# Masked attention and a mixture of attention heads on one core: the weights' jobs five units further up, 65-wide slices of V, and a refitted order

## The chip, the cores and the metric

The kernel runs on one core of a Trainium2 chip. What is compared is device time in microseconds (us): the median of several runs of one launch. Times of single instructions come from one profiled execution.

## The reference, cut to what matters

```python
def reference(q, k, v, proj, w_gate, wq, wk, wv, wo):   # q, k, v: 4 x 8 x 768 x 64
    qb, kb = bucket(q @ proj), bucket(k @ proj)          # 6 sign bits each
    s = where(qb[..., :, None] == kb[..., None, :], q @ k.T / 8, -1e9)
    x = softmax(s) @ v                                   # 4 x 8 x 768 x 64
    x = x.transpose(0, 2, 1, 3).reshape(4, 768, 512)
    w, topk = softmax over the best 2 of 4 of x @ w_gate
    out = 0
    for e in range(4):                                   # wq, wk, wv: 4 x 512 x 64
        a = softmax(causal((x @ wq[e]) @ (x @ wk[e]).T / 8))
        out += (w of e, where e is in topk) * (a @ (x @ wv[e]) @ wo[e])
    return out                                           # 4 x 768 x 512
```

## The kernel before, in words

**Units.** The work is a list `seq` of 48 units: 32 of the masked attention (`L`, one per batch and head) and 16 of the mixture (`M`, one per batch and expert). A unit's scores are 768 x 768, made transposed in chunks of up to 512 columns: TensorE writes scores to PSUM (`st`), ScalarE takes their exponential twice, into `p` (float32) and `ph` (float16), GpSimd or VectorE writes the rest `pl` = p - ph, and TensorE multiplies by V in three matmuls per 128 x 128 block: `o<-vh,ph`, `o<-vl,ph`, `o<-vh,pl` (V too is split, `vh` + `vl`). VectorE then divides by the denominators into `xp` (`yn` in the mixture). Two units ahead TensorE makes the scores once more the other way round (`mx`), and VectorE reduces them to each row's maximum (`pm`, `pmw`), which goes by way of a small transposed row (`row`, `roww`) and a DMA into the scores' operand.

**Jobs beside the units.** Loads of a pair of heads (`natq`, `natk`, `natv`), their scales (`mqk`), their float16 halves (`qk`, `xt`), the hash signs (TensorE `misc<-qk,pbh` and `misc<-qk,pbl`, matmuls of 32 columns of weights that run four side by side in column groups; VectorE `M`), the preparation of V (`vf`, `vh`, `vl`, `vcol`, `vr`), the transposes of x (`xt`) and the mixture's projections. `load_weights` is a generator of nine steps: it stages the expert weights in `wst`, takes their largest magnitudes (`qkmax`, `mw`) on VectorE, scales them on ScalarE (`wst<-wst,cw`), and writes halves (`wqk_h`, `wvg_h`, `wo_h` on ScalarE, `wqk_l`, `wvg_l`, `wo_l` on GpSimd). The main loop counts units from -6; from unit `W0` on it runs one step of that generator per unit.

**What sets the order.** All operations are recorded first, in the loop's order. `schedule()` is a list scheduler: it gives each engine its instructions in the order of the recorded position plus a number for the operation's group out of the table `PLACE`, by a planner that costs each kind of operation from the table `TIMES` and waits by `LAT` and `LATE`. Some operations may go to either of two engines, and the planner chooses. `issue()` then emits them, so that in the profile every instruction carries one line (L716 before). Engines run their queues in order; SP (SyncE) issues nearly all DMAs. Fillers (`o<-ident`) are matmuls at the start, whose result nobody uses. Each of the three `st` tiles is one PSUM bank, and so are the two `misc`, the two `mx` and the one `o`.

**V's slices before.** A pair's V tile holds [unused, ones, V of head 0, V of head 1, ones] in 132 columns. Head 1 took the 65 columns from 66 on (V, ones); head 0 took 66 columns from 0 on, with V two columns in, so that its `o<-vl,ph` wrote from column 66i + 2 of the PSUM tile.

Of the kernel before, what the change touches and what calls it, by code (L numbers as in the profile page):

```python
# [133 lines left out]
class Op:  # L134
# [133 lines left out]
scalar activation lg misc 4 4 PS 151 258 0 0 0
scalar activation misc gw 24 24 SP 130 194 0 0 0
scalar activation misc lg 24 24 SP 102 197 0 0 0  # L270
scalar activation mvh misc 256 256 PS 276 383 0 0 0
scalar activation ot misc 512 512 PS 576 687 0 0 0
# [7 lines left out]
scalar activation pf st 512 512 PS 478 607 0 0 0  # L280
scalar activation ph st 256 256 PS 263 419 0 0 0
scalar activation ph st 384 384 PS 370 503 0 0 0
scalar activation ph st 512 512 PS 477 605 0 0 0
scalar activation qk misc 384 384 PS 372 490 0 0 0
scalar activation qk natk 384 384 SS 501 640 0 0 0
scalar activation qk natk 768 768 SS 895 1015 0 0 0
scalar activation qk natq 384 384 SS 498 619 0 0 0
scalar activation qk natq 768 768 SS 895 1015 0 0 0
scalar activation row misc 128 128 PS 158 256 0 0 0
scalar activation roww misc 128 128 PS 167 258 0 0 0  # L290
scalar activation rw cw 1 1 SS 147 242 0 0 0
scalar activation vcol misc 1 1 PS 53 178 0 0 0
scalar activation vf natv 384 384 SS 507 625 0 0 0
scalar activation vh vf 384 384 SS 419 550 0 0 0
# [170 lines left out]
class Recorder:  # L465
# [102 lines left out]
    def schedule(self):  # L568
# [39 lines left out]
        while left:  # L608
# [1285 lines left out]
```

## Time and profile before

| | |
|---|---|
| median of 3 runs | 607.84 us (606.49 to 609.29) |
| profiled execution, its own time | 609.53 us |
| its span, first to last instruction | 607.8 us (1.7 us of the time lie outside) |
| mean granted TensorE clock | 0.994 |
| busy, share of the span: PE, DVE, ACT, POOL | 98%, 82%, 83%, 76% |

PE is TensorE, PEld its weight loads, DVE VectorE, ACT ScalarE, POOL GpSimd. Matmuls overlap each other, so PE's busy time is time in which at least one is under way; how fast they follow one another is read from their starts.

### The profile page before, as it was taken

To read this page: it belongs to the slowest core of one execution; us is meant where nothing else is said; L and a number is where in the kernel's file an instruction comes from. 1 tells how busy PE (TensorE), PEld (TensorE's weight loads), DVE (VectorE), ACT (ScalarE), POOL (GpSimd) and SP (SyncE) were. 2 spreads that over 40 slices of the span, in tenths; PEclk is the share of its full clock that TensorE was granted. 3 is DMA by queue.
4 is the path that set the end of the run, shared out by engine and by line. 5 is a ranking of instruction groups with operands and counts; after the bars stand their busy time and mean duration, and the time that the engine had idled before them with its cause. 6 is when DMAs were issued, how large, how long until landed. Compare 5 with 4: busy or idle time off the path is not lost.

```text
span 607.8 us, 20469 instructions
## 1 busy us (share of the span) xinstructions
PE 593.4 (98%) x7850; PEld 429.4 (71%) x7850; DVE 499.0 (82%) x1374; ACT 502.1 (83%) x1075; POOL 463.1 (76%) x520
## 2 busy tenths in 40 slices
PE   8899999999999999999999999999999999999996
PEld 6567876667677776777776676767766767767673
DVE  5896889999899899988989789987979794557853
ACT  6586999999888899977997899887978978954683
POOL 9476798999965989985896689867996778951550
PEclk9997999999999999999999999999999999999999
DMA  5652064150422115131324314141033121011222
GB/s 170 164 166 67 9 173 138 42 151 18 140 80 94 45 42 138 25 115 42 105 61 131 104 44 132 28 132 35 19 124 99 50 63 28 11 27 43 57 89 104
DMA packets 38967, 50.24 MB, mean 83 GB/s; under 512 B 13226, under 2 KB 27350, under 8 KB 38870
## 3 DMA queue, kind: packets, MB, share of 16 engines
q1 hardware_dynamic: 38870, 48.95, 28.6%
q8 instruction: 61, 1.00, 0.7%
q14 instruction: 36, 0.29, 0.1%
HBM read 20.98 MB, written 6.29 MB: 45 GB/s over the span
## 4 chain that ended last, share of the span: by engine, by line
PE 83%; DVE 6%; ACT 5%; DMA 2%; issue 2%; POOL 1%; SPq 1%; ACTq 0%; POOLq 0%; DVEq 0%
PE misc L716 25%; PE st L716 25%; PE o L716 21%; PE mx L716 13%; ACT ph L716 2%; DVE pm L716 1%; ACT p L716 1%; DMA natv<-in_v_dram 1%; POOL pl L716 1%; DVE qk L716 1%; DVE xt L716 1%; SPq L716 1%; DMA wst<-in_moe_wk_dram 1%; DVE misc L716 1%; DMA xt<-roww 0%
## 5 line engine op out<-in xcount | busy, mean ns | idle before, releaser
L716 POOL TENSOR_TENSOR pl<-p,ph 128x512 f16<-128x512 f32 x367 | 409.0, 1141 | 116.6 <-ACT ph L716 44.6
L716 ACT ACTIVATE p<-st 128x512 f32<-128x512 f32 x372 | 227.7, 616 | 30.2 <-PE st L716 24.2
L716 PE MATMUL st<-qk 78*128 78x512 f16 (+3 forms) x976 | 228.1, 324 | 0.4
L716 ACT ACTIVATE ph<-st 128x512 f16<-128x512 f32 x372 | 228.0, 621 | 0.6 <-PE o L716 0.4
L716 DVE TENSOR_REDUCE pm<-mx 128x2 f32<-128x512 f32 (+2 forms) x284 | 186.9, 675 | 16.4 <-PE mx L716 15.2
L716 PEld LDWEIGHTS <-ph 128*128 128x128 f16 x2880 | 157.2, 98 | 25.0 <-DVE xp L716 1.5
L716 PEld LDWEIGHTS <-qk 128*128 128x128 f16 (+5 forms) x1560 | 130.0, 98 | 56.6 <-issue 7.0
L716 PEld LDWEIGHTS <-pl 128*128 128x128 f16 x1440 | 132.5, 97 | 9.8 <-POOL pl L716 4.2
L716 PE MATMUL mx<-qk 76*128 76x512 f16 (+2 forms) x488 | 135.6, 325 | 1.9 <-DVE pm L716 1.0
L716 PE MATMUL o<-vh,ph 128*128 128x65 f16 (+1 forms) x1104 | 126.9, 194 | 2.1 <-DVE xp L716 1.0
L716 PE MATMUL o<-vl,ph 128*128 128x64 f16 x1104 | 126.6, 192 | 0.1
L716 PE MATMUL o<-vh,pl 128*128 128x65 f16 (+1 forms) x1104 | 125.3, 194 | 0.5 <-POOL pl L716 0.3
L716 PE MATMUL misc<-xt,wqk_h 128*128 128x384 f16 x256 | 57.7, 325 | 0.2 <-DVE qk L716 0.2
L716 DVE CUSTOM_DVE_ANT_0 spare<-mx,causal 128x512 bf16<-128x512 f32 (+2 forms) x96 | 44.3, 461 | 9.3 <-PE mx L716 7.4
L716 PE MATMUL o<-mvh,pl 128*128 128x65 f16 x336 | 37.4, 193 | 0.8 <-POOL pl L716 0.8
L716 PEld LDWEIGHTS <-xt 128*128 128x128 f16 x324 | 30.3, 97 | 10.8 <-ACT xt L716 0.5
L716 PE MATMUL o<-mvh,ph 128*128 128x65 f16 x336 | 37.6, 194 | 0.0
L716 PE MATMUL o<-mvl,ph 128*128 128x64 f16 x336 | 37.6, 192 | 0.0
L716 PEld LDWEIGHTS <-wqk_h 128*128 128x128 f16 x256 | 24.1, 98 | 14.6 <-issue 0.3
L716 POOL TENSOR_TENSOR vl<-vf,vh 128x384 f16<-128x384 f32 x32 | 29.3, 925 | 6.0 <-DVE qk L716 2.6
L716 ACT ACTIVATE qk<-misc 128x384 f16<-128x384 f32 x26 | 13.0, 500 | 20.4 <-PE misc L716 20.2
L716 PE MATMUL misc<-wvg_h,xt 128*128 128x260 f16 x192 | 29.7, 274 | 0.0
(198 smaller groups left out, 902.9 us busy)
## 6 DMA issues: line engine op xcount, KB each, us to landing
qk<-qk SPq DMA_DIRECT2D x128, 96.0 KB
natv<-in_v_dram SPq DMA_DIRECT2D x16, 384.0 KB
qk<-qk SPq DMA_DIRECT2D x32, 192.0 KB
natq<-in_q_dram SPq DMA_DIRECT2D x15, 384.0 KB
natk<-in_k_dram SPq DMA_DIRECT2D x15, 384.0 KB
out_dram<-ot SPq DMA_DIRECT2D x20, 256.0 KB
xt<-xt SPq DMA_DIRECT2D x4, 192.0 KB
out_dram<-p SPq DMA_DIRECT2D x3, 256.0 KB
```

Of the source, the lines that this page charges most:

```text
L716: o.made = getattr(getattr(self.nc, e), m)(*[real(x) for x in args], **{k: real(x) for k, x in kw.items()})
```

## The change

The weights' generator starts at unit -2 and not 3. Both heads take V in slices 65 wide: head 0 from column 1 (ones, V), so that its moving operand starts at an odd float16 and its `o<-vl,ph` writes from column 66i + 1. All numbers of `PLACE` are new, and `TIMES` is measured anew (most entries move by a few per cent; a matmul in column groups falls from 60 to 40 ns). The planner counts what it costs TensorE to enter or leave the column groups (`TURN`), lets GpSimd wait out a VectorE operation that it is made to follow, and scales a landing's delay by the tile.

```diff
-W0 = 3
+W0 = -2
+TURN = 97.0
+CLASH = 0
-tensor matmul dt.float16 384 - g 60 326 0 0 0
+tensor matmul dt.float16 384 - g 40 326 0 0 1
...
+                    if e == "tensor" and mode and not a[4][4]:
+                        pen += TURN
...
-                st += pen if o.wide else 0.0
-                last = busy
+                st += pen + (TURN if port > mode else 0.0)
+                last, mode = busy, port
...
-                o.end += LATE
+                of = o.ins[0].tile.name.rstrip("0123456789_") if o.ins else ""
+                o.end += LATE * (1.5 if of in ("M", "Mw") else 0.4 if of in ("row", "roww", "fr", "vr", "rows") else 1.0)
...
                 if half is not None and hold[0] + 100.0 < st:
                     o.after, half = half, None
-                if hold[1] - 130.0 > st and hold[0] < st + 80.0:
+                    st = max(st, hold[1] + LAT[e])
+                elif hold[1] - 130.0 > st and hold[0] < st + 80.0:
                     st = hold[1] - 130.0
...
-            U["L", b, 2 * hp + h].update(vf=vf[:, :, 66 * h:66 * h + 66], vh=vh[:, :, 66 * h:66 * h + 66], vl=vl[:, :, h], first=2 - 2 * h, den=64 * h,
-                                         order=[2 * (i % 3) + i // 3 for i in range(NT)], c=c, vs=vs[:, h])
+            w = slice(1 + 65 * h, 66 + 65 * h)
+            U["L", b, 2 * hp + h].update(vf=vf[:, :, w], vh=vh[:, :, w], vl=vl[:, :, h], first=1 - h, den=64 * h,
+                                         order=[2 * (i % 3) + i // 3 for i in range(NT)], c=c, vs=vs.rearrange("p h d -> p (h d)")[:, w])
...
-                        w = 66 if f else 65
-                        oa, ol = O[:, 66 * i:66 * i + w], O[:, 66 * i + f:66 * i + f + 64]
+                        oa, ol = O[:, 66 * i:66 * i + 65], O[:, 66 * i + f:66 * i + f + 64]
```

The instructions stay the same in number but for 12 more fillers and some copies that change between VectorE and ScalarE. Their order is new on every engine. Three places show it.

On SP, the first DMAs after the first loads; `xt<-roww` carries the row maxima on which the first score chunk waits. Before:

```order
L716 DMA xt<-xt 64x384 x2
L716 DMA qk<-qk 64x384 x4
L716 DMA xt<-xt 64x768 x2
L716 DMA xt<-xt 64x384 x2
L716 DMA natv<-in_v_dram 128x768
L716 DMA xt<-roww 1x6x128
```

After:

```order
L720 DMA xt<-xt 64x384 x2
L720 DMA wst<-in_moe_wq_dram 128x4x64
L720 DMA qk<-qk 64x384 x4
L720 DMA xt<-xt 64x768 x2
L720 DMA xt<-xt 64x384
L720 DMA wst<-in_moe_wk_dram 128x4x64
L720 DMA natv<-in_v_dram 128x768
L720 DMA wst<-in_moe_wq_dram 128x4x64
L720 DMA xt<-xt 64x384
L720 DMA wst<-in_moe_wk_dram 128x4x64
L720 DMA xt<-roww 1x6x128
```

Four of the eight loads of wq and wk now stand between the start's own DMAs, ahead of `xt<-roww`; before, all eight stood behind the loads of a later pair of heads.

On VectorE, the place of the reductions `qkmax`. Before, they lie around the normalisation (`xp`) of the fifth masked unit, some 150 rows into the queue:

```order
L716 TENSOR_SCALAR rden<-o,cs_529 128x6
L716 RECIPROCAL cs_1846<-misc 128x1
L716 TENSOR_SCALAR negh_167<-misc 128x12
L716 RECIPROCAL rden<-rden 128x6
L716 TENSOR_REDUCE qkmax<-wst 128x2
L716 TENSOR_TENSOR xp<-o,rden 128x6x64
L716 TENSOR_REDUCE qkmax<-wst 128x2
L716 SCALAR_TENSOR_TENSOR qk<-natq,cs_1846,qk 128x2x384
```

After, they begin some fifteen rows into the queue, between the row maxima (`pmw`) of the second unit:

```order
L720 COPY least_times<-misc 128x3
L720 TENSOR_REDUCE pmw_184<-mx 128x2 x2
L720 TENSOR_REDUCE misc<-misc 128x1
L720 TENSOR_REDUCE qkmax<-wst 128x2
L720 TENSOR_SCALAR Mw<-misc,least_times 128x384
L720 TENSOR_REDUCE pmw_184<-mx 128x2
L720 TENSOR_SCALAR misc<-misc 128x1
```

So `xp` no longer stands behind a reduction of the weights, and the start's row maxima do.

On TensorE, the hash signs of a pair of heads (`misc<-qk,pbh` and `pbl`, 12 matmuls; the weight loads between them are single rows). Before, one such run is broken in two by a matmul of `mx` and a transpose of `vcol`:

```order
L716 MATMUL misc<-qk,pbl 32x384
L716 LDWEIGHTS pbl
L716 MATMUL misc<-qk,pbl 32x384
L716 LDWEIGHTS qk
L716 MATMUL mx<-qk 128x512
L716 MATMUL misc<-ident,vcol 1x128
L716 LDWEIGHTS pbl
L716 MATMUL misc<-qk,pbl 32x384
L716 LDWEIGHTS pbh
L716 MATMUL misc<-qk,pbh 32x384
```

After, the 12 stand together; this is the end of one run:

```order
L720 MATMUL misc<-qk,pbl 32x384
L720 LDWEIGHTS pbl
L720 MATMUL misc<-qk,pbl 32x384
L720 LDWEIGHTS pbh
L720 MATMUL misc<-qk,pbh 32x384
L720 LDWEIGHTS pbh
L720 MATMUL misc<-qk,pbh 32x384
L720 LDWEIGHTS qk
L720 MATMUL mx<-qk 128x512
```

In the whole program the column-group matmuls stand in 22 runs before and in 17 after.

## Rows read from the trace of the kernel before

**Rows 1.** Windows: length, then PE, PEld, DVE, ACT, POOL busy us, PEclk, DMA share, GB/s.
```profile
0.00:52.00 52.00, 46.92 (x446) 33.58 (x447) 42.51 (x92) 34.84 (x79) 34.51 (x111) 0.95 0.56 158
52.00:80.00 28.00, 28.00 (x421) 22.53 (x419) 21.22 (x54) 24.86 (x52) 23.42 (x21) 0.96 0.15 43
80.00:130.00 50.00, 47.28 (x685) 34.32 (x682) 47.87 (x110) 48.09 (x101) 45.77 (x43) 1.00 0.45 123
130.00:197.00 67.00, 66.69 (x878) 49.68 (x877) 61.68 (x182) 60.34 (x142) 54.05 (x54) 1.00 0.32 88
197.00:560.00 363.00, 361.55 (x4959) 261.15 (x4957) 299.23 (x852) 302.23 (x639) 285.84 (x275) 1.00 0.25 68
560.00:608.00 48.00, 42.97 (x478) 28.17 (x475) 26.45 (x87) 31.79 (x70) 19.51 (x19) 0.99 0.25 84
```

**Rows 2.** Chain of waits, 78 to 98 us: start, length, what.
```profile
89.25 4.28 DMA wst<-in_moe_wk_dram
93.55 0.69 DVE qkmax L716
94.24 0.47 DVE xp L716
94.76 1.25 PE o L716 x36
```

**Rows 3.** Operations on the staged weights: count, ns least/median/most, first and last start.
```profile
L716 ACT ACTIVATE wst<-wst,cw x18: 280/552/706, 109.3 to 174.9; 128x256 f32<-128x256 f32 x12, 128x4 f32<-128x4 f32 x4, 128x512 f32<-128x512 f32 x2
L716 SPq DMA_DIRECT2D wst<-in_moe_wq_dram x4: 505/546/657, 86.2 to 90.8; - x4
...
L716 DVE TENSOR_REDUCE qkmax<-wst x4: 664/674/686, 93.6 to 100.9; 128x2 f32<-128x512 f32 x4
L716 ACT ACTIVATE wqk_h<-wst x4: 633/713/766, 110.9 to 134.3; 128x512 f16<-128x512 f32 x4
L716 POOL TENSOR_TENSOR wqk_l<-wst,wqk_h x4: 1157/1158/1162, 112.6 to 135.8; 128x512 f16<-128x512 f32 x4
...
L716 ACT ACTIVATE wvg_h<-wst x4: 402/402/403, 143.8 to 147.4; 128x260 f16<-128x260 f32 x4
L716 POOL TENSOR_TENSOR wvg_l<-wst,wvg_h x4: 680/684/686, 146.5 to 149.4; 128x260 f16<-128x260 f32 x4
```

**Rows 4.** Windows at the start, columns as in rows 1.
```profile
10.00:50.00 40.00, 37.02 (x349) 25.87 (x348) 37.13 (x83) 26.57 (x61) 25.29 (x26) 0.97 0.53 145
```

**Rows 5.** Timeline of TensorE at its first scores: start, us, instruction, idle before.
```profile
20.07 0.50 PE L716 MATMUL st<-xt 77*128 77x512 f32 x1 [0.71 <-DMA xt<-roww]
```

**Rows 6.** Timeline of TensorE around a whole run in column groups.
```profile
157.59 0.35 PE L716 MATMUL misc<-qk,pbh 128*32 128x384 f16 x4
...
158.20 0.39 PE L716 MATMUL st<-qk 78*128 78x512 f16 x1
```

**Rows 7.** Timeline of TensorE around the run that is broken in two.
```profile
97.43 0.35 PE L716 MATMUL misc<-qk,pbh 128*32 128x384 f16 x4
...
97.87 0.39 PE L716 MATMUL mx<-qk 76*128 76x512 f16 x1
...
98.30 0.34 PE L716 MATMUL misc<-qk,pbl 128*32 128x384 f16 x1
...
98.73 0.39 PE L716 MATMUL mx<-qk 76*128 76x512 f16 x1
```

**Rows 8.** Timeline of TensorE at head 0's matmuls with V.
```profile
200.08 0.19 PE L716 MATMUL o<-vh,ph 128*128 128x66 f16 x1
200.11 0.20 PE L716 MATMUL o<-vl,ph 128*128 128x64 f16 x1
```

**Rows 9.** Waits: us in total, times, longest.
```profile
POOL pl L716 <- DVE qk L716: 10.9, 6, 4.3
...
PEld L716 <- POOL pl L716: 4.2, 13, 0.7
```

**Rows 10.** Windows at the clock's fall, columns as in rows 1.
```profile
47.00:54.00 7.00, 7.00 (x79) 6.01 (x79) 4.12 (x10) 4.29 (x11) 2.91 (x4) 0.52 0.37 87
```

More of the change, by code (lines that the diff above doesn't have):

```diff
@@ L226 @@
 gpsimd memset mask_t - 128 1 SS 154 204 0 0 0
-gpsimd memset mvh - 48 1 SS 84 141 0 0 0
+gpsimd memset mvh - 48 1 SS 83 134 0 0 0
 gpsimd memset negh - 128 1 SS 141 194 0 0 0
 gpsimd memset negm - 72 1 SS 90 148 0 0 0
-gpsimd memset one - 2 1 SS 97 175 0 0 0
+gpsimd memset one - 2 1 SS 104 175 0 0 0
 gpsimd memset ones - 2 1 SS 49 99 0 0 0
@@ L261 @@
 gpsimd tensor_tensor wo_l wst 512 512 SS 1119 1157 0 0 0
-gpsimd tensor_tensor wqk_l wst 512 512 SS 1121 1159 0 0 0
-gpsimd tensor_tensor wvg_l wst 260 260 SS 637 675 0 0 0
-gpsimd tensor_tensor xt natk 384 384 SS 954 992 0 0 0
+gpsimd tensor_tensor wqk_l wst 512 512 SS 1119 1157 0 0 0
+gpsimd tensor_tensor wvg_l wst 260 260 SS 636 674 0 0 0
+gpsimd tensor_tensor xt natk 384 384 SS 956 994 0 0 0
 gpsimd tensor_tensor xt natq 384 384 SS 955 993 0 0 0
 scalar activation Tq o 512 512 PS 592 687 0 0 0
-scalar activation identh ident 128 128 SS 214 310 0 0 0
@@ L268 @@
[L268 to L272, printed above, removed]
+scalar activation identh ident 128 128 SS 214 309 0 0 0
+scalar activation lg misc 4 4 PS 150 258 0 0 0
+scalar activation misc gw 24 24 SP 123 194 0 0 0
+scalar activation misc lg 24 24 SP 101 196 0 0 0
+scalar activation mvh misc 256 256 PS 274 383 0 0 0
@@ L280 @@
[L280 removed]
+scalar activation pbh pbs 64 64 SS 156 251 0 0 0
+scalar activation pbs pbd 64 64 SS 251 346 0 0 0
+scalar activation pf st 512 512 PS 478 606 0 0 0
 scalar activation ph st 256 256 PS 263 419 0 0 0
[L282 to L294, printed above, removed]
-scalar activation vr misc 128 128 PS 164 258 0 0 0
-scalar activation wo_h wst 512 512 SS 570 664 0 0 0
@@ L297 @@
-scalar activation wqk_h wst 512 512 SS 522 647 0 0 0
-scalar activation wst wst 256 256 SS 399 520 0 0 0
-scalar activation wst wst 4 4 SS 188 312 0 0 0
-scalar activation wst wst 512 512 SS 671 766 0 0 0
-scalar activation wvg_h wst 260 260 SS 309 443 0 0 0
-scalar activation xs xw 1 1 SS 186 297 0 0 0
-scalar activation xt misc 384 384 PS 463 588 0 0 0
-scalar activation xt natk 384 384 SS 476 522 0 0 0
-scalar activation xt natq 384 384 SS 480 522 0 0 0
-scalar activation xw misc 1 1 PS 62 172 0 0 0
@@ L307 @@
-scalar activation yth misc 256 256 PS 263 400 0 0 0
+scalar activation ph st 384 384 PS 370 505 0 0 0
+scalar activation ph st 512 512 PS 477 608 0 0 0
+scalar activation qk misc 384 384 PS 375 490 0 0 0
+scalar activation qk natk 384 384 SS 480 608 0 0 0
+scalar activation qk natk 768 768 SS 826 957 0 0 0
+scalar activation qk natq 384 384 SS 477 592 0 0 0
+scalar activation qk natq 768 768 SS 828 950 0 0 0
+scalar activation row misc 128 128 PS 158 259 0 0 0
+scalar activation roww misc 128 128 PS 166 258 0 0 0
@@ new lines @@
+scalar activation rw cw 1 1 SS 133 228 0 0 0
+scalar activation vcol misc 1 1 PS 55 177 0 0 0
+scalar activation vf natv 384 384 SS 507 628 0 0 0
+scalar activation vh vf 384 384 SS 419 546 0 0 0
+scalar activation vr misc 128 128 PS 162 261 0 0 0
+scalar activation wo_h wst 512 512 SS 556 651 0 0 0
+scalar activation wqk_h wst 512 512 SS 521 658 0 0 0
+scalar activation wst wst 256 256 SS 399 531 0 0 0
+scalar activation wst wst 4 4 SS 188 304 0 0 0
+scalar activation wst wst 512 512 SS 656 750 0 0 0
@@ L308 @@
+scalar activation wvg_h wst 260 260 SS 309 433 0 0 0
+scalar activation xs xw 1 1 SS 186 294 0 0 0
+scalar activation xt misc 384 384 PS 464 591 0 0 0
+scalar activation xt natk 384 384 SS 482 522 0 0 0
+scalar activation xt natq 384 384 SS 484 522 0 0 0
+scalar activation xw misc 1 1 PS 64 172 0 0 0
+scalar activation yth misc 256 256 PS 264 396 0 0 0
 scalar reg_load scale cs 1 1 SS 120 120 0 0 0
@@ L310 @@
 sync - Tq 0 378 333 1680 660 0
-sync - ot 0 510 344 1680 660 0
-sync - p 0 425 382 1680 660 0
-sync fq fr 768 784 701 1090 -400 0
-sync natk - 1536 458 417 2700 1200 0
-sync natk - 768 465 431 2000 550 0
-sync natq - 1536 485 433 2700 1200 0
+sync - ot 0 531 344 1680 660 0
+sync - p 0 426 383 1680 660 0
+sync fq fr 768 773 701 1090 -400 0
+sync natk - 1536 462 418 2700 1200 0
+sync natk - 768 466 431 2000 550 0
+sync natq - 1536 483 433 2700 1200 0
 sync natq - 768 460 432 2000 550 0
-sync natv - 1536 515 432 2700 1200 0
+sync natv - 1536 499 431 2700 1200 0
 sync pst - 12 477 432 1600 200 0
-sync qk M 768 893 827 1260 170 0
-sync qk Mw 1536 906 841 1480 300 0
-sync qk qk 1536 562 535 2060 557 0
-sync qk qk 768 613 535 1580 278 0
-sync qk row 768 792 707 1090 -400 0
-sync qk rows 768 870 807 1090 -400 0
-sync qk roww 1536 805 764 1090 -400 0
-sync vs vr 132 765 672 1103 170 0
-sync wst - 1024 748 580 2790 794 0
-sync wst - 512 578 550 1945 397 0
-sync wst - 8 636 536 1300 170 0
-sync xt roww 1536 847 771 1090 -400 0
-sync xt xt 1536 611 547 2060 557 0
-sync xt xt 768 612 554 1580 278 0
-tensor matmul dt.bfloat16 1 misc - 67 164 0 0 0
+sync qk M 768 895 829 1260 170 0
+sync qk Mw 1536 905 841 1480 300 0
+sync qk qk 1536 582 535 2060 557 0
+sync qk qk 768 628 537 1580 278 0
+sync qk row 768 789 710 1090 -400 0
+sync qk rows 768 873 802 1090 -400 0
+sync qk roww 1536 794 757 1090 -400 0
+sync vs vr 132 757 671 1103 170 0
+sync wst - 1024 702 539 2790 794 0
+sync wst - 512 570 508 1945 397 0
+sync wst - 8 613 503 1300 170 0
+sync xt roww 1536 849 771 1090 -400 0
+sync xt xt 1536 612 546 2060 557 0
+sync xt xt 768 616 578 1580 278 0
+tensor matmul dt.bfloat16 1 misc - 67 166 0 0 0
 tensor matmul dt.bfloat16 128 misc - 56 219 0 0 0
@@ L356 @@
-vector reciprocal gm misc 6 6 PS 157 188 0 0 0
-vector reciprocal misc xs 1 1 SP 120 161 0 0 0
-vector reciprocal o rden 6 6 SP 146 194 0 0 0
-vector reciprocal rden rden 6 6 SS 133 186 0 0 0
-vector reciprocal rw misc 3 3 PS 100 178 0 0 0
+tensor matmul dt.float32 384 misc g 190 599 0 0 1
+tensor matmul dt.float32 65 o - 206 387 0 0 0
+tensor matmul dt.float32r 256 mx - 163 321 0 0 0
+tensor matmul dt.float32r 256 st - 142 284 0 0 0
+tensor matmul dt.float32r 512 mx - 323 490 0 0 0
+tensor matmul dt.float32r 512 st - 268 410 0 0 0
@@ L361 @@
+tensor transpose dt.float32 128 - - 108 272 0 0 0
+vector reciprocal cs misc 1 1 PS 82 158 0 0 0
+vector reciprocal gm misc 6 6 PS 146 188 0 0 0
+vector reciprocal misc xs 1 1 SP 127 161 0 0 0
+vector reciprocal o rden 6 6 SP 154 194 0 0 0
+vector reciprocal rden rden 6 6 SS 140 186 0 0 0
+vector reciprocal rw misc 3 3 PS 98 176 0 0 0
 vector scalar_tensor_tensor misc gcnt 24 24 PP 135 182 0 0 0
-vector scalar_tensor_tensor mvl misc 256 256 PS 338 418 0 0 0
-vector scalar_tensor_tensor negh misc 6 6 PS 89 159 0 0 0
+vector scalar_tensor_tensor mvl misc 256 256 PS 341 420 0 0 0
@@ L387 @@
-vector tensor_reduce mw qkmax 2 8 SS 68 146 0 0 0
-vector tensor_reduce mw wst 1 1024 SS 1130 1206 0 0 0
-vector tensor_reduce mw wst 1 16 SS 77 155 0 0 0
-vector tensor_reduce mx natv 1 768 SS 856 934 0 0 0
-vector tensor_reduce mx pst 1 6 SS 61 139 0 0 0
-vector tensor_reduce negm pmw 12 48 SS 119 196 0 0 0
-vector tensor_reduce pm mx 1 384 PS 463 548 0 0 0
-vector tensor_reduce pm mx 1 512 PS 628 682 0 0 0
-vector tensor_reduce pm mx 2 512 PS 600 681 0 0 0
-vector tensor_reduce pmw mx 2 512 PS 609 682 0 0 0
@@ L397 @@
-vector tensor_reduce qkmax wst 2 512 SS 585 666 0 0 0
-vector tensor_reduce xs cs 1 4 SS 104 150 0 0 0
-vector tensor_scalar M misc 384 384 PS 603 674 0 0 0
-vector tensor_scalar Mw misc 384 384 PS 597 675 0 0 0
+vector tensor_copy vcol misc 1 1 PS 91 149 0 0 0
+vector tensor_copy vr misc 128 128 PS 201 273 0 0 0
+vector tensor_copy xt misc 384 384 PS 479 557 0 0 0
+vector tensor_copy yth misc 256 256 PS 349 424 0 0 0
+vector tensor_reduce gcnt misc 24 96 PS 207 250 0 0 0
+vector tensor_reduce gm misc 6 24 PS 154 176 0 0 0
@@ new lines @@
+vector tensor_reduce misc misc 1 128 PP 207 288 0 0 0
+vector tensor_reduce misc misc 2 256 PP 343 424 0 0 0
+vector tensor_reduce misc misc 3 384 PP 487 556 0 0 0
+vector tensor_reduce misc misc 6 24 PP 126 184 0 0 0
+vector tensor_reduce misc pm 6 24 SP 145 180 0 0 0
+vector tensor_reduce mqk natk 1 768 SS 913 946 0 0 0
+vector tensor_reduce mqk natq 1 768 SS 884 946 0 0 0
+vector tensor_reduce mqk natv 1 768 SS 858 946 0 0 0
+vector tensor_reduce mw qkmax 2 8 SS 62 140 0 0 0
+vector tensor_reduce mw wst 1 1024 SS 1130 1209 0 0 0
@@ new lines @@
+vector tensor_reduce mw wst 1 16 SS 78 156 0 0 0
+vector tensor_reduce mx natv 1 768 SS 856 934 0 0 0
+vector tensor_reduce mx pst 1 6 SS 62 140 0 0 0
+vector tensor_reduce negm pmw 12 48 SS 118 198 0 0 0
+vector tensor_reduce pm mx 1 384 PS 465 548 0 0 0
+vector tensor_reduce pm mx 1 512 PS 620 682 0 0 0
+vector tensor_reduce pm mx 2 512 PS 601 682 0 0 0
+vector tensor_reduce pmw mx 2 512 PS 610 682 0 0 0
+vector tensor_reduce qkmax wst 2 512 SS 589 669 0 0 0
+vector tensor_reduce xs cs 1 4 SS 99 149 0 0 0
@@ L430 @@
-vector tensor_tensor misc gate 96 96 SP 210 262 0 0 0
-vector tensor_tensor misc misc 96 96 PP 249 266 0 0 0
+vector tensor_tensor gate misc 96 96 PS 214 256 0 0 0
+vector tensor_tensor gw misc 24 24 PS 176 179 0 0 0
+vector tensor_tensor misc gate 96 96 SP 211 262 0 0 0
+vector tensor_tensor misc misc 96 96 PP 253 266 0 0 0
 vector tensor_tensor pl p 256 256 SS 320 400 0 0 1
@@ L676, in schedule @@
                 free[e], o.end = st + busy, st + lasts
-            elif port:
+            elif port and e == "vector":
                 o.end = st + lasts
@@ L1435, in f @@
                         if pl is None:
-                            nc.tensor.matmul(oa, ph[:, o:o + 128], d["vf"][:, d["order"][j], 0:w], start=first, stop=False,
+                            nc.tensor.matmul(oa, ph[:, o:o + 128], d["vf"][:, d["order"][j], 0:65], start=first, stop=False,
                                              skip_group_check=True)
@@ L1439, in f @@
                             continue
-                        nc.tensor.matmul(oa, ph[:, o:o + 128], d["vh"][:, d["order"][j], 0:w], start=first, stop=False,
+                        nc.tensor.matmul(oa, ph[:, o:o + 128], d["vh"][:, d["order"][j], 0:65], start=first, stop=False,
                                          skip_group_check=True)
@@ L1443, in f @@
                                          skip_group_check=True)
-                        nc.tensor.matmul(oa, pl[:, o:o + 128], d["vh"][:, d["order"][j], 0:w], start=False, stop=last and not lsh,
+                        nc.tensor.matmul(oa, pl[:, o:o + 128], d["vh"][:, d["order"][j], 0:65], start=False, stop=last and not lsh,
                                          skip_group_check=True)
@@ L1449, in f @@
                         for i in range(NT):
-                            nc.tensor.matmul(O[:, 66 * i:66 * i + w], d["fq"][0:FR0 + 2, i * 128:(i + 1) * 128],
-                                             d["vs"][0:FR0 + 2, 0:w], start=False, stop=i == NT - 1, skip_group_check=True)
+                            nc.tensor.matmul(O[:, 66 * i:66 * i + 65], d["fq"][0:FR0 + 2, i * 128:(i + 1) * 128],
+                                             d["vs"][0:FR0 + 2], start=False, stop=i == NT - 1, skip_group_check=True)
                     nc.tag, nc.job = "norm", ("norm", u)
```

137 lines of the change are left out of this document (57 added, 80 removed), and 78 rows, old and new, of the table PLACE.

## The prediction

> **What bounds the kernel now.** I read the windows by stage first [rows 1]. From 130 us on TensorE binds: 66.69 of 67 us busy, then 361.55 of 363, while the next engine is at 61.68 and 302.23. What any other engine saves there is worth nothing until TensorE waits for it. From 80 to 130 us three engines lie close together, ScalarE at 48.09, VectorE at 47.87 and GpSimd at 45.77 of 50, and TensorE has 2.72 us with nothing under way: here the other engines bind. From 52 to 80 us TensorE is busy throughout, and the others have room (VectorE 6.8 us, GpSimd 4.6, ScalarE 3.1). The start idles TensorE for 5.1 us and the tail for 5.0. At the start it is VectorE that is full: from 10 to 50 us it is busy 37.13 of 40 us, ScalarE 26.57 [rows 4].
>
> Then the chain of waits around 90 us [rows 2]: a load of the weights lands 4.28 us after its issue, `qkmax` reduces it, `xp` stands behind `qkmax` in VectorE's queue, and TensorE's next product with V waits for `xp` (which frees the one `o` tile). So the weights' jobs are on the path there, in the one stretch where TensorE has idle time to give back.
>
> Last the small things: what a run in column groups costs [rows 6, 7], how fast the matmuls with V follow one another [rows 8], what GpSimd waits for [rows 9], and the clock [rows 10].
>
> **The change part by part.** The basis is the profiled execution, 609.53 us, 1.7 us above the median; the sum is taken off the first and then set down to the second.
>
> 1. *The weights' jobs, out of 80 to 130 us.* The steps on wq and wk lie between 86 and 136 us now [rows 3]: on VectorE four `qkmax` of 0.674 us, 2.7; on ScalarE eight of the `wst` scalings at 0.552 and four `wqk_h` at 0.713, 7.3; on GpSimd four `wqk_l` of 1.158, 4.6. Five units earlier puts `qkmax` into the first 50 us (the order shows it in VectorE's fifteenth row), and scalings and halves from some 62 us on, which is the stretch with room. But the generator's next steps move up as well: those on wv and the gate stand at 132 to 149 us now and come into the stretch that has just been emptied. ScalarE gets four scalings at 0.552, four narrow ones at 0.280 and four `wvg_h` at 0.402 [rows 3], 4.9 us; GpSimd four `wvg_l` of 0.684, 2.7; VectorE a reduction of 1024 columns, by `qkmax`'s 512 columns some 1.3. Net, the stretch loses 2.4 us on ScalarE, 1.9 on GpSimd and 1.4 on VectorE. ScalarE is the fullest, so I take 2.4 us off. The upper bound is TensorE's idle time there, 2.72, and some of what hides between pipelined matmuls, together 5; the lower is nothing, if VectorE or the wait for a projection's operand sets the pace. **-2.4 (0 to -5).** That contains the chain at 94 us: `qkmax`'s 0.69 and its wait go.
>
> 2. *The same jobs, into the start.* VectorE, the engine that binds there, gets up to 2.7 us of `qkmax`, and SP four issues of some 0.55 us [rows 3], 2.2 us, ahead of `xt<-roww`, on which the first score matmul waits at 20.07 with TensorE idle for 0.71 us [rows 5]. In VectorE's queue row maxima stand behind the reductions, behind those the scores of the second unit, and for them ScalarE waits. For cover: the first `mx` matmuls, which followed those scores, now stand ahead of them; and the 52 to 80 us stretch has room to catch up, as long as TensorE isn't the one delayed. If nothing covers, the whole 2.7 counts; if everything does, nothing. I take **+1 (0 to +2.7)**, for the fuller the engine, the less is hidden, but two of the four reductions come late enough to meet the room.
>
> 3. *Column groups.* A run of 12 takes 0.61 us from its first matmul to the next ordinary one (157.59 to 158.20, [rows 6]). The one that is broken in two takes 0.44 and 0.43 (97.43 to 97.87, 98.30 to 98.73, [rows 7]), 0.87 together, so one break costs 0.26 us. There are five runs fewer. All on TensorE, which mostly binds: 5 x 0.26 = **-1.3 (-0.5 to -1.8)**; less, since one of them stands in the start, where TensorE idles anyway.
>
> 4. *65 wide for 66.* Head 0's matmuls start 30 ns apart, the 66-wide one no later than the 64-wide one ([rows 8]: 200.08, 200.11). One column of 66 is 1.5% of 30 ns, 0.45 ns; some 1,220 matmuls become narrower, 0.5 us at most, and nothing if the pitch is not set by columns. **-0.3 (0 to -0.5).**
>
> 5. *GpSimd's waits in the planner.* GpSimd waits 10.9 us for VectorE's `qk`, and TensorE waits 4.2 us for `pl` [rows 9]. A planner that counts that wait can set other work in it. GpSimd isn't the bound after 130 us, so only part of TensorE's 4.2 is at stake: **-0.5 (0 to -4.2).**
>
> 6. *A new order everywhere else.* Each change of order moves waits about that nothing here prices. I take nothing for it, and 3 us either way in the range: the size of TensorE's idle time in one stretch [rows 1].
>
> 7. *The clock.* [...] The new start has other gaps and 12 more fillers. It may lose the fall, keep it, or fall twice; I take it as unchanged, with 3.4 us to either side.
>
> Sum: -2.4 + 1 - 1.3 - 0.3 - 0.5 = -3.5, so 606.0 for the profiled execution; less 1.7, **604.3 us**.
>
> [...] In every row of before, head 0's `o<-vl,ph` writes from an even float32 word of PSUM, so the trace shows no odd start; the row has 30 ns from one matmul to the next [rows 8]. [...]
>
> **The rivals.**
>
> *Slower: the weights' work lands where nothing has room.* Place: the queue of VectorE from 20 to 50 us, and ScalarE around 62 to 85 us. ScalarE has 3.1 us of room in 52 to 80 and gets up to 7.3; 4.2 would be left over, and VectorE's 2.7 at the start come first. If the scores of the fourth to sixth units come that much later and the emptied stretch, bound by VectorE as much as by ScalarE, gives nothing back, the sum is 607.84 + 2.7 + 4.2 - 1.3 - 0.3 = 613. It decides as soon as TensorE shows over 3 us more idle time before 85 us than now. For it: the start's VectorE at 93%. Against: ScalarE's room before 50 us, 13 us of 40.
>
> *No change: the stall moves.* TensorE binds 430 of the 608 us, its work is the same, and the mixture's projections can't begin before the last masked unit of the first batch is through; work that is ready earlier then waits. Parts 1 and 2 cancel, parts 3 and 4 are worth 1.6 at most: 607.8 - 1 = 607, within 2 of it. For it: after 130 us only 0.31 and 1.45 us are visibly idle [rows 1].
>
> [...]
>
> *Faster by more:* the half-clock stretch goes too, or part 1 gives its 5: some 599 to 601.
>
> **How the numbers follow.** The forecast's own case (602 to 606) has 0.36, the larger gain 0.15, no change 0.28, the first slower rival 0.16, the odd start 0.05. The measurement can't tell less than about 0.5% from no change, 3 us, so the bounds are 604.8 and 610.9. Faster by more than that: two thirds of the forecast's case, the larger gain, and a little of the second rival, whose runs spread, 0.45. Slower: both slower rivals and a refit that misses, 0.21. The rest, 0.34. The range for 8 in 10 takes in the larger gain down to 598 and the first slower rival up to 612.5, and leaves out the odd start and the ends. The likeliest case's own range is 602 to 606.
>
> **What would show it.** In the changed kernel's windows from 80 to 130 us (or the same units) ScalarE should be 2 us less busy and TensorE's idle time under 1.5 us, with no `qkmax` in the chain at `xp`. At the start the first `st<-xt` should come 1.5 to 2.2 us later than 20.07, with `mx` ahead of it and no more than 1 us of further idle time by 52 us. Whole column-group runs should still take 0.61 us, with none broken. Head 0's matmuls should be 30 ns apart. I would be wrong if the stretch at half clock grows or vanishes, if TensorE waits before 85 us on ScalarE's `ph`, or if after 197 us the new order takes more or less than 363 us for the same matmuls by over 2 us.

## The result, and the profile after

The changed kernel takes 613.07 us (median of 8 runs, 609.96 to 613.77), the kernel before 609.11 us in the same rounds (606.49 to 610.75). The ratio is 1.0063 with a 95% interval of 1.0041 to 1.0085: slower by 0.6%, where 0.6% faster was forecast, and just above the range's upper end of 612.5. Seven of the 8 runs have a mean granted clock of 0.979 to 0.983 and take 612.4 to 613.8 us; the one at 0.992 took 609.96.

The windows of the changed kernel, with the columns of [rows 1]: length, busy us of PE, PEld, DVE, ACT and POOL, granted clock, DMA share, GB/s. The last three are other cuts of the start, one of them that of [rows 4].

```profile
0.00:52.00 52.00, 46.23 (x405) 35.08 (x405) 38.11 (x85) 31.98 (x71) 33.20 (x111) 0.84 0.55 150
52.00:80.00 28.00, 26.87 (x343) 21.54 (x344) 23.88 (x59) 25.99 (x57) 21.74 (x21) 0.88 0.34 91
80.00:130.00 50.00, 48.17 (x717) 36.05 (x716) 47.67 (x114) 48.73 (x107) 45.34 (x44) 1.00 0.38 107
130.00:197.00 67.00, 66.59 (x873) 50.00 (x873) 57.73 (x164) 54.57 (x121) 50.95 (x48) 1.00 0.23 65
197.00:560.00 363.00, 362.30 (x5011) 263.06 (x5010) 302.10 (x848) 306.05 (x652) 292.14 (x281) 1.00 0.26 72
...
10.00:50.00 40.00, 36.49 (x311) 27.49 (x312) 32.05 (x74) 21.72 (x48) 21.90 (x25) 0.79 0.56 145
23.00:39.00 16.00, 16.00 (x67) 11.29 (x67) 9.90 (x24) 10.57 (x22) 7.79 (x8) 0.50 0.49 131
54.00:60.00 6.00, 6.00 (x57) 4.26 (x56) 3.82 (x9) 4.44 (x13) 0.95 (x2) 0.50 0.21 67
```

The seventh number is the one to read. Before, TensorE was at the lower level (a granted clock of 0.50) for some 7 us of the start, 0.52 over the window of [rows 10]; now it is there for some 17 us around the window from 23 to 39, and for 7 more around that from 54 to 60, 0.50 over both. From 23 to 39 us TensorE is busy throughout and VectorE only 9.90 of 16 us: the engine that bound the start [rows 4] no longer does. From 80 us on the clock and TensorE's share are those of before, or better.

What TensorE did ahead of the fall, in its timeline (start, us, instruction, idle time before it):

```profile
15.93 1.95 PE L720 MATMUL o<-ident 128*128 128x128 bf16 x32
18.95 0.70 PE L720 MATMUL mx<-xt 76*128 76x512 f32 x3 [1.07 <-DVE xt L720]
19.59 0.22 PE L720 MATMUL misc<-one,pat 1*128 1x1 bf16 x3
19.76 0.23 PE L720 MATMUL misc<-ident,mx 128*128 128x128 bf16 x1
22.00 1.21 PE L720 MATMUL st<-xt 77*128 77x512 f32 x4 [2.01 <-DMA xt<-roww]
```

The fillers end at 17.9 us, TensorE waits 1.07 us for `mx`'s operand, works for 1.0 us, and waits 2.01 us for `xt<-roww`. Before, 38 fillers ran from 17.07 to 19.36, and the first score waited 0.71 us behind them, until 20.07 [rows 5]:

```profile
17.07 2.29 PE L716 MATMUL o<-ident 128*128 128x128 bf16 x38
```

SP's own timeline says why `xt<-roww` is late:

```profile
16.33 0.59 SPq L720 DMA_DIRECT2D wst<-in_moe_wk_dram  x1
16.96 0.57 SPq L720 DMA_DIRECT2D natv<-in_v_dram  x1
17.57 0.46 SPq L720 DMA_DIRECT2D wst<-in_moe_wq_dram  x1
18.12 0.47 SPq L720 DMA_DIRECT2D xt<-xt  x1
18.64 0.59 SPq L720 DMA_DIRECT2D wst<-in_moe_wk_dram  x1
19.32 0.85 SPq L720 DMA_DIRECT2D xt<-roww  x1
```

It is issued at 19.32, behind weight loads at 16.33, 17.57 and 18.64 (a fourth stands at 10.30).

**Where the time went.** To compare programs whose order differs I added up TensorE's instructions in order, each with the usual step to the next start of its kind (the 20th percentile over one trace, the same for all; fillers left out), and asked when a given amount of this work was reached. In us later than the kernel before, whose profiled execution holds its own 7 us at the lower clock:

```
work done, us       25     50     80    190    530
(before, at)      50.9   79.1  113.8  231.3  587.3
changed           +7.6   +8.1   +6.3   +6.5   +3.9
fill              +4.2   +4.4   +2.6   +2.8   +0.2
dma               +3.9   +4.3   +2.5   +2.5   -0.2
nat               +2.8   +2.9   +1.3   +1.0   -1.6
mw_even           +1.8   +2.0   +0.1   -0.2   -3.4
slices            -1.4   -2.5   -2.5   -2.2   -1.2
```

The changed kernel loses 8 us by 80 us and then gains 4: 1.8 between 50 and 80 us of work, which is the stretch that the weights left, and 2.6 after 190. The names are those of the experiments below.

Two things in these rows are the executions' own. The first `mx` matmul, ahead of the edits of these runs, starts at 8.88 us before, 8.53 in the changed kernel, 8.94 in `dma`, 9.03 in `nat`, but at 9.96 in `fill` and 9.69 in `mw_even`; so 1.1 us of `fill`'s delay against before and 0.8 of `mw_even`'s arise ahead of anything compared here. And the profiles differ in falls of the clock: those of `mw_even` and `slices` hold none before the last few us. `slices` is the old order without a fall, and against it `mw_even` is 4.5 us late at 50 us of work.

### The profile page after: what moved, and what is told of

It is laid out like the page before. It is cut to its first block, busy times and chain, and to the rows that moved or that the text cites. A ratio compares the mean times of both kernels' runs of the same rounds, so it can differ in the third digit from the quotient of the medians.

```text
span 611.5 us, 20504 instructions
## 1 busy us (share of the span) xinstructions
PE 597.4 (98%) x7862; PEld 437.7 (72%) x7862; DVE 498.5 (82%) x1368; ACT 501.7 (82%) x1079; POOL 464.8 (76%) x522
## 4 chain that ended last, share of the span: by engine, by line
PE 86%; DVE 5%; ACT 3%; POOL 3%; issue 1%; DMA 1%; SPq 0%; ACTq 0%; DVEq 0%; POOLq 0%
PE st L720 27%; PE misc L720 25%; PE o L720 22%; PE mx L720 13%; DVE pm L720 2%; DVE qk L720 1%; ACT ph L720 1%; ACT p L720 1%; POOL xt L720 1%; POOL qk L720 1%; DVE misc L720 0%; SPq L720 0%; DMA xt<-roww 0%; POOL pl L720 0%; DMA qk<-qk 0%
## 5 line engine op out<-in xcount | busy, mean ns | idle before, releaser
L720 PEld LDWEIGHTS <-ph 128*128 128x128 f16 x2880 | 163.3, 98 | 28.0 <-DVE xp L720 1.0
L720 PEld LDWEIGHTS <-pl 128*128 128x128 f16 x1440 | 134.1, 98 | 9.1 <-issue 1.9
L720 PE MATMUL o<-vh,ph 128*128 128x65 f16 x1104 | 131.0, 196 | 0.2 <-DVE xp L720 0.2
L720 PE MATMUL o<-vh,pl 128*128 128x65 f16 x1104 | 130.3, 195 | 0.2 <-POOL pl L720 0.2
L720 PE MATMUL o<-vl,ph 128*128 128x64 f16 x1104 | 129.9, 193 | 0.0
L720 PE MATMUL misc<-xt,wqk_h 128*128 128x384 f16 x256 | 55.7, 326 | 0.0
L720 ACT ACTIVATE qk<-misc 128x384 f16<-128x384 f32 x29 | 14.5, 499 | 27.5 <-PE misc L720 27.3
L720 PE MATMUL misc<-wvg_h,xt 128*128 128x260 f16 x192 | 31.3, 274 | 0.0
```

What stands on the lines that cost most here:

```text
L720: o.made = getattr(getattr(self.nc, e), m)(*[real(x) for x in args], **{k: real(x) for k, x in kw.items()})
```

## The experiments

The second `xp`, the end of the normalisation of the second masked unit, serves as a mark of how late the start is: 60.7 us before, 69.6 in the changed kernel. Two theories at first. **Clock:** the idle time ahead of the first score lets the granted clock fall, and the time at the lower level is the loss. **Work:** the weights' jobs in the start's queues are the loss by themselves. A third, **order:** the refitted order is slower all along. Each round also ran the kernel before; ratios are to it, with 95% intervals.

**fill**: the changed kernel's order, with fillers in the two gaps.

```diff
+MORE = {("max", ("L", 0, 1)): 20, ("qk", ("L", 0, 0)): 36}
...
+                    for _ in range(MORE.pop(o.job, 0)):
+                        order.append((self.filler[0], self.filler[1]))
```

> The changed kernel, in its own order, with 20 more filler matmuls ahead of the mx at 18.95 us and 36 more ahead of the first score matmul at 22.00, so that TensorE doesn't sit idle there; the wait for the row maxima stays as it is. Clock theory (the idle time lets the granted clock fall, and 16 us at half the clock are the loss): full clock from 23 to 39 us, the second xp within 2 us of the kernel before's 60.7 instead of 69.7, and 604 to 608 in all. Work theory (the weights' jobs themselves make the start late): the clock may stay, but the second xp comes at 67 or later, 611 to 614. Order theory (the refitted order is slower all along): 611 to 614.

607.66 us, ratio 0.998 (0.9963 to 0.9998), 5.4 us less than the changed kernel by matmuls whose result nobody uses. The first score came no earlier, at 23.24 (1.24 us later, in a profile whose first `mx` is 1.43 later), but the clock stayed up until 35:

```profile
23.00:34.00 11.00, 10.32 (x70) 6.95 (x68) 9.84 (x26) 9.13 (x20) 5.99 (x6) 1.00 0.67 182
34.00:40.00 6.00, 5.14 (x74) 4.76 (x73) 4.33 (x8) 2.37 (x7) 5.17 (x5) 0.72 0.76 198
```

It isn't all: the second `xp` came at 65.9, not near 60.7. Clock theory holds for the larger part, and some 3 us of the start stay, 4.4 less the 1.1 ahead of the first `mx`.

**dma**: the order as it was, but the four `wst` loads moved behind `xt<-roww` on SP (the finished order is edited; no planning anew).

```diff
...
+        behind(lambda o: o.job[:1] == ("weights",) and o.eng == "sync", lambda o: of(o, "sync", "xt", "roww"))
```

> The changed kernel in its own order on every engine but SP, where the four wst loads that stood ahead of xt<-roww follow it. Clock theory, if SP's issues are what makes TensorE idle: the first score matmul at 20 to 20.3 us instead of 22.0, idle time before it under 0.5 us, no fall of the clock at 23, 605 to 608 in all. If the fall comes from the idle time of 1.07 us ahead of the mx at 18.95, which stays: clock half from 21 to 37 us as in the changed kernel, 610 to 613.

609.06 us, ratio 1.0008 (0.9992 to 1.0024), 4.0 us less than the changed kernel, but above the 605 to 608 expected. The first score started at 20.20, and the stretch that was at half the clock is at the full clock, though the 1.07 us ahead of `mx` stayed. So moving four loads on SP was enough to avoid the long fall:

```profile
20.00:24.00 4.00, 3.85 (x26) 2.42 (x25) 3.97 (x9) 1.90 (x4) 1.16 (x1) 1.00 0.86 193
24.00:39.00 15.00, 11.62 (x124) 8.66 (x124) 12.12 (x31) 10.21 (x24) 9.98 (x10) 1.00 0.63 177
```

Its timelines show the next loss, VectorE waiting for a load and TensorE for VectorE:

```profile
33.87 0.95 DVE L731 TENSOR_REDUCE mqk<-natq 128x1 bf16<-128x768 f32 x1 [2.47 <-DMA natq<-in_q_dram]
...
36.25 0.23 PE L731 MATMUL misc<-ident,mqk 128*128 128x128 bf16 x1 [1.14 <-DVE mqk L731]
```

`natq` of the third pair was issued at 28.84, before at 20.36, since it now stood behind the weights and `qk<-Mw`.

**roww_late**: the test from the other side, the kernel *before* with two `xt<-xt` moved ahead of `xt<-roww` on SP and nothing else.

```diff
...
+        r = next(i for i, (o, _) in enumerate(order) if of(o, "sync", "xt", "roww"))
+        j = [i for i, (o, _) in enumerate(order) if i > r and o.eng == "sync"][1]
+        order[:] = order[:r] + order[r + 1:j + 1] + [order[r]] + order[j + 1:]
```

> The kernel before in its own order, but that xt<-roww follows two xt<-xt on SP, 1.2 us later. Clock theory, from the other side: TensorE idles some 1.9 us instead of 0.7 ahead of the first score, the clock falls there as in the changed kernel, and the time is 612 to 615. Work theory: the 1.2 us are covered or shift the start by that much, 609 to 610.5, clock as before.

614.28 us, ratio 1.0065 (1.0041 to 1.0088): as slow as the changed kernel. Eight of 12 runs had a mean clock of 0.984 to 0.986 and 613.7 to 615.1 us; the run at 0.998 took 608.55. The profiled one, at 0.994 and 611.30 us, escaped the early fall:

```profile
17.84 2.30 PE L729 MATMUL o<-ident 128*128 128x128 bf16 x38
21.81 0.50 PE L729 MATMUL st<-xt 77*128 77x512 f32 x1 [1.67 <-DMA xt<-roww]
```

So where the clock fell in the eight runs isn't on record. By their mean clock, against 0.994 before, they spent some 11 us more at the lower level (an estimate: 2 x 0.009 x 612 us, as the lower level reads 0.50 in the traces), and most executions with this gap lost the clock, not all. The runs without that loss give the delay by itself: 608.55 for 606.9 at 0.998, 1.7 us of the 4.7, which leaves some 3 for the clock.

**nat_late**: the kernel before with `natq` and `natk` of the third pair behind `qk<-Mw`.

```diff
...
+        order[:] = [x for i, x in enumerate(order[:j + 1]) if i not in q] + [order[i] for i in q] + order[j + 1:]
```

> The kernel before in its own order, but that natq and natk of the third pair follow the four qk<-Mw on SP, at about 28.4 us instead of 20.4, as they do in the changed kernel. If these loads are the second cause: VectorE waits for them at some 33 us, TensorE for mqk, 611 to 613. If the changed kernel's wait is due to the wst loads that share the DMA engines: 609 to 610.

611.42 us, ratio 1.0034 (1.0015 to 1.0052), with the same wait and no weights near it:

```profile
30.68 0.95 DVE L731 TENSOR_REDUCE mqk<-natq 128x1 bf16<-128x768 f32 x1 [2.85 <-DMA natq<-in_q_dram]
```

**nat**: `dma`, with `natq` and `natk` right behind `fq<-fr`.

> The kernel called dma (wst loads behind xt<-roww), with natq and natk of the third pair of heads issued right behind fq<-fr, at about 21 us instead of 28.8; no other engine's order changes. In dma VectorE waits 2.5 us for natq at 33.9 and TensorE 1.1 and 0.6 us for mqk at 36 to 37. If these two loads are what is left of the start's loss: those waits go, the second xp comes 2.5 to 4 us earlier than in dma, 605 to 607 in all. If VectorE's qkmax or the later Mw is: within 1 us of dma's 609.06.

608.04 us, ratio 0.9983 (0.9959 to 1.0007), short of the 605 to 607 expected. The waits for `natq` went, the second `xp` came 1.7 us earlier, less than expected: TensorE now waited for the next DMA in SP's queue, `qk<-Mw`, which four more weight loads hold up (they are issued from 23.71 to 26.59, `qk<-Mw` from 27.21 on).

```profile
31.25 0.47 PE L740 MATMUL mx<-qk 76*128 76x512 f32 x1 [1.65 <-DMA qk<-Mw]
```

The clock fell behind that wait, at 33 us (0.80 from 32 to 34, 0.50 from 34 to 40). At equal clock it is ahead: its runs at 0.994 took 607.1 to 607.9, those of the kernel before 608.8 to 610.8.

**slices**: the kernel before, every engine's order unchanged, with the 65-wide slices alone.

```diff
+            w = slice(1 + 65 * h, 66 + 65 * h)
+            U["L", b, 2 * hp + h].update(vf=vf[:, :, w], vh=vh[:, :, w], vl=vl[:, :, h], first=1 - h, den=64 * h,
...
```

> The kernel before, in its own order instruction by instruction, with the 65-wide slices of V alone. If an odd start costs head 0's 552 products their pace (60 ns for 30), some 17 us more than before, about 626. If the width sets the pitch, 0.3 to 0.5 us less. If neither, no difference that can be measured, 608 to 610.

610.06 us, ratio 1.0014 (0.9992 to 1.0035): the doubling is excluded, the gain not seen. At equal clock it is behind: its four runs at 0.993 and 0.994 took 610.4 to 611.0, the mean of the kernel before's there is 609.9. Its profiled execution had no fall at all (clock 0.999), against the 7 us of [rows 10] in the same order: that fall comes in some executions and not in others, and the runs of the kernel before lie mostly at 606 to 608 us without it (clock 0.998 and up) and near 610 at 0.994.

**mw** and **mw_even**: `nat`, with the last four weight loads behind `qk<-Mw` and the third `qkmax` beside the fourth; and the same with head 0's slices as before. The edit between the two, with the widths that follow from it; the order is the same on every engine:

```diff
-            w = slice(1 + 65 * h, 66 + 65 * h)
+            U["L", b, 2 * hp + h].update(vf=vf[:, :, 66 * h:66 * h + 66], vh=vh[:, :, 66 * h:66 * h + 66], vl=vl[:, :, h], first=2 - 2 * h, den=64 * h,
...
```

> The kernel called nat, with the last four wst loads behind the four qk<-Mw on SP as well (these are issued at about 24.3 us instead of 27.2), and the third qkmax, which needs one of those loads, beside the fourth on VectorE. In nat TensorE waits 1.65 us for qk<-Mw at 31.25. If the place of the weights' loads on SP is all of the start's loss: that wait goes, the second xp at 61 to 62.5 us instead of 64.2, 604 to 606.5 in all. If the rest lies in VectorE's queue: the wait moves to another row, within 1 us of nat's 608.04.

608.58 us, ratio 0.9995 (0.9977 to 1.0013). The wait for `qk<-Mw` shrank to about 0.9 us, but the second `xp` stayed at 64.2, and its runs spread with the clock, from 606.6 to 607.8 at 0.997 to 611.6 at 0.982. SP is thus not all of what is left.

> The same, with head 0's slices of V as before (66 wide, even). If head 0's steps of 33.7 against 31.6 ns cost 1.2 us: 0.5 to 1.5 us less than mw. If not: the same within 0.5 us.

**605.97 us, ratio 0.9946 (0.9927 to 0.9965): faster than both kernels**, with a clock of 0.996 to 1.0 in six of 7 runs. At 0.997 it took 605.1 and 606.0, `mw` 606.6 to 607.8, so some 1.6 us belong to the slices and the rest of the 2.6 to the clock. Against the kernel before, too, the clock is part of the 3.2 us: at 1.0 `mw_even` took 605.1 to 606.1, the kernel before 607.1 twice, so some 1.6 us are left at equal clock. Single rows of the timeline, here of the changed kernel at head 0, don't show the step:

```profile
205.87 0.19 PE L720 MATMUL o<-vh,ph 128*128 128x65 f16 x1
205.90 0.20 PE L720 MATMUL o<-vl,ph 128*128 128x64 f16 x1
205.93 0.19 PE L720 MATMUL o<-vh,pl 128*128 128x65 f16 x1
...
206.11 0.19 PE L720 MATMUL o<-vh,ph 128*128 128x65 f16 x1
206.14 0.20 PE L720 MATMUL o<-vl,ph 128*128 128x64 f16 x1
206.17 0.19 PE L720 MATMUL o<-vh,pl 128*128 128x65 f16 x1
```

They are rounded to 10 ns, and 30 ns apart as in [rows 8]. Over some 1,000 steps of head 0 after 150 us their mean is 29.9 ns before, 30.7 in `slices`, 30.6 in the changed kernel and 29.9 in `mw_even`, while head 1 keeps 29.9 in all four. Over head 0's 1,656 products (three times 552) that is 0.75 x 1.656 = 1.2 us. In `slices` the lengthening lies in the step from `vh,ph` to `vl,ph`, 33.7 ns for 31.6 before; the step from `vh,pl` to the next `vh,ph`, which both read V from an odd float16, is 29.5 for 29.4. That speaks for the odd column that `o<-vl,ph` writes and against the odd operand, but no run has one without the other.

**all**, **both** and **best** were earlier tries at a version that beats both. `both`: `dma`, with fillers, and all four `qkmax` moved down to stand ahead of `mw`. `all`: the same with even slices. `best`: `nat` with even slices and 43 fillers in three places.

> Both moves (wst loads behind xt<-roww, qkmax late) with 20 fillers ahead of the mx, 18 ahead of the first score and 18 ahead of the first product with V. If the changed kernel's loss lies wholly in these places of its start: second xp at 60 to 62 us, 602 to 604 in all. If the rest of the new order is no faster than before's, 606 to 609.

> The same, with head 0's slices of V as they were before (66 wide, V from an even column). In the kernel before with the new slices alone, head 0's step from vh,ph to vl,ph grew from 31.6 to 33.7 ns on average; over 552 of them that is 1.2 us. If the odd start costs that, the step goes back to 31 to 32 ns and the time lies 0.5 to 1.5 us below the one of both; if not, the two are the same.

> The kernel called nat, with head 0's slices as before (66 wide, even) and 20, 9 and 14 more fillers ahead of the mx at 19, the first score and the first product with V. If the odd start costs 2 ns in each of head 0's steps and the other repairs hold, 604 to 606, below both kernels. If only nat's moves count, the same as nat.

611.08 (1.0024 to 1.0060), 610.55 (1.0008 to 1.0052) and 609.39 us (0.9974 to 1.0019), all short of what was expected of them; `all` lies 0.5 us below `both`, which is within the noise. The likely reason for the first two is in **qlate**, which moves the four `qkmax` alone in `fill`:

```diff
...
+        k = next(i for i, (o, _) in enumerate(order) if of(o, "vector", "mw", "qkmax"))
+        late = [x for x in order[:k] if of(x[0], "vector", "qkmax", "wst")]
...
```

> The changed kernel with the 56 fillers, and the four qkmax moved down VectorE's queue to stand ahead of mw, behind the start's row maxima. If VectorE's 2.7 us are what makes the start of the filled kernel 3 to 5 us late: the second xp 2 to 3 us earlier than in the filled kernel (65.9), 605 in all at the median. If VectorE had room between its waits: within 1 us of the filled kernel's 607.66 and of its second xp.

612.3 us, ratio 1.0068 (1.0043 to 1.0093), 4.6 more than `fill`. Early in the queue the reductions cost less than bunched: there TensorE waited 1.98 us for the negated row maxima (`negm`) behind them, and the clock was down from 47.5 to 57.8 (0.50 from 48 to 56).

```profile
47.08 0.30 PE L735 MATMUL misc<-ident,negm 128*72 128x128 f32 x1 [1.98 <-DVE negm L735]
```

In `best` a wait of 2.11 us for `qk<-Mw`, until 31.96, stayed, with a fall behind it (0.50 from 32 to 38 us); its fillers bought nothing there.

**behind** (the first weight steps held until the first unit's row maxima, planned anew) and **late** (`W0` back at 3, each number of the table kept with its operations, planned anew):

```diff
-        if i >= W0:
-            nc.gate = marks["m"]
+        for w in (-2, -1, 0) if not i else (i,) if i > 0 else ():
+            nc.gate = marks["row"] if w < 0 else marks["m"]
...
-W0 = -2
+W0 = 3
```

> The changed kernel with the first two steps of the weights behind the first unit's row maxima: the wst loads follow xt<-roww on SP; the planner orders the rest anew with the same table, so some thousand rows of TensorE's order move. Clock theory: the first score matmul at 20.0 to 20.5 us, no idle time over 1 us before it, full clock up to 39 us, 603 to 608. Work theory: qkmax and the wst loads still lie in the start, 610 to 613. Order theory: 610 to 614.

> The changed kernel with W0 back at 3, each group of the table kept with its operations; so the new planner, slices and table without the weights' move. Clock theory and work theory both: the start is as before, the second xp at 60 to 63 us, 604 to 609. Order theory: as slow as the changed kernel, 611 to 614.

617.55 (1.0091 to 1.0149) and 634.92 us (1.0345 to 1.0422), and neither time decides what it was made for. With the same table but other jobs the planner moved over a thousand rows of TensorE's order, and other falls of the clock came: from 43 to 61 (0.50) and 136 to 142 us in `behind`, from 22 to 39, 49 to 63 and 196 to 206 (0.50 in all three) in `late`. The table fitted to one program didn't carry to its neighbours; the edits of the finished order do tell parts apart.

The profile of `late` does bear on the clock theory. No weight load stands in its start, the first score follows `mx` without a gap, and yet the clock fell at 21.8 us for as long as in the changed kernel, with 1.07 us ahead of `mx` as the last idle time before it:

```profile
20.02 0.70 PE L963 MATMUL mx<-xt 76*128 76x512 f32 x3 [1.07 <-DVE xt L963]
...
21.00 1.01 PE L963 MATMUL st<-xt 77*128 77x512 f32 x4
```

```profile
22.00:38.00 16.00, 16.00 (x100) 12.50 (x100) 12.14 (x27) 11.13 (x25) 9.45 (x10) 0.50 0.41 119
```

The same 1.07 us stand in `dma`, `nat`, `mw` and `mw_even`, whose profiles keep the full clock there. So a gap of that length can come before a long fall too. What the 2.01 us add is told by the mean clocks: 0.979 to 0.983 in seven of the changed kernel's 8 runs, 0.986 to 0.994 in all 12 of `dma`.

## Why the prediction was wrong

**Part 2, the start, failed: +1 (0 to +2.7) was said, and with the clock some 8 was measured.** Its mechanism was right as far as it went: four issues ahead of `xt<-roww`, 1.93 us later first score (22.00 for 20.07), as forecast. The step that failed is "for cover: the first `mx` matmuls now stand ahead of them". With what follows them they last 1.0 us and end at 20 us; behind them TensorE had nothing, and the fillers stood before them. I priced the wait by its length and not by what it does to the clock. `fill`, whose profile is at the lower level for as long as the kernel before's, some 7 us, is still some 3 us late: that is part 2's own term, above its range, and the other 5 are the clock's.

**Part 7, the clock, taken as unchanged within 3.4 us, failed with it.** The 3.4 us are an estimate from [rows 10], 7.00 us x (1 - 0.52). The prediction's own sign of being wrong, that the stretch at half clock grows, came true: 24 us at the lower level (0.50) in place of 7. `fill` prices the early fall at 5.4 us, and `roww_late`, its delay included, at 4.7. The trace has 2.01 us of waiting for `xt<-roww` ahead of the fall at 22.6 us; how long a wait has to be for the clock to fall is not shown. I had a stretch at half clock among my rows and no row for what a new gap would do.

**Left out of part 2: the other DMAs behind the weight loads.** I counted four issues against `xt<-roww` alone. `natq` and `natk` stood 8.7 us later, and `nat_late` prices such a delay at 2 us in the old kernel; then came `qk<-Mw`. VectorE's added `qkmax`, which I named as the price, were not shown to cost anything where they stood.

**The first rival named the right sign and the wrong place.** Its price (613) was met by luck, and not by ScalarE at 62 to 85 us and VectorE's load: VectorE had room at 23 to 39 us (busy 9.90 of 16), and TensorE's waits for ScalarE's `ph` before 85 us came to 1.2 us, for 0.2 before. Its sign of TensorE's idle time before 85 us over 3 us more than before wasn't met either: 6.9 us in the first two windows against 5.1; the rest was slow work, not idleness.

**Part 1 came near its number, not by its mechanism:** -2.4 forecast, 1.8 us gained between 50 and 80 us of work, with `qkmax` gone from the chain at `xp`. But ScalarE isn't 2 us less busy from 80 to 130 us (48.73 for 48.09), since other work came in, and TensorE's idle time there fell from 2.72 to 1.83, not under 1.5. That the weights' leaving made the gain is read from its place; no run has that move alone.

**Part 3 was right in kind:** the column-group runs after 80 us are whole and take 0.6 us (one 0.7); four breaks of about 0.27 us are gone after 97 us, 1.1 us of the 1.3.

**Part 4 had the wrong sign:** +1.2 us for -0.3. The odd start, which has 0.05 among the chances and some 17 us in the expectation of `slices`, exists at a fourteenth of that price. That it doubles the step was my supposition, and no run shows it; `slices` shows 30.7 ns for 29.9, 0.75 ns per step: so little is it here.

**Parts 5 and 6** aren't separated. Part 5's waits of [rows 9] did shrink, GpSimd's for `qk` from 10.9 to 5.4 us and TensorE's for `pl` from 4.2 to 1.2, but no run says what that gave in time:

```profile
POOL pl L720 <- DVE qk L720: 5.4, 5, 1.2
...
PEld L720 <- POOL pl L720: 1.2, 4, 0.5
```

After 190 us of work the changed kernel gains 2.6 us in spite of the slices, `mw_even` 3.2: the refitted order is better by some 3 us where TensorE binds. Most of that is the uncertainty of part 6, or part 5, come out as a gain. The order theory falls with it.

What stays open: why some executions with the same gap keep the clock, and the delay that is left in the start of `mw_even`, 4.5 us at 50 us of work against `slices` (some 3.6 without what lies ahead of the first `mx`).

## What to carry to other kernels

Price a wait of TensorE twice: by its length, and by the clock behind it (here 2.01 us, and some 17 us at 0.50). Fillers paid here where they stood in the gap itself (`fill`, 5.4 us); in `roww_late` 38 of them ran until the gap began, and most runs lost the clock (0.984 to 0.986 in eight of 12). When loads are moved up SP's queue, go through every transfer that stands behind them, not the first alone: here the first score, behind `xt<-roww`, started 1.93 us later, and `natq` was issued 8.7 us later. Compare runs by their mean clock before a difference of half a per cent is given to an edit, and take effects apart by editing the finished order.

## What the runs showed of the hardware

With V read from an odd float16 and `o<-vl,ph` written from an odd float32 word of PSUM, between two products that write from an even one, the mean step of head 0's products went from 29.9 ns in the kernel before to 30.7 in `slices`. At the start, a gap of 2.01 us was followed by some 17 us at half the clock (0.50) in the changed kernel and one of 1.07 us likewise in `late`; one of 1.67 us in `roww_late`, and the same 1.07 us in `dma`, by none at once. And one and the same program, the kernel before, lay at 606.3 to 611.8 us over its runs, those at a mean clock of 0.998 and up mostly at 606 to 608, those at 0.987 to 0.989 at 610.6 to 611.8.
